# A transformer block on one core: feed-forward products taken in pairs that share one weight load

## The chip, the core and the metric

The kernel runs on one core of a Trainium2 chip. The core has a matrix engine (TensorE; in the profile PE for its products and PEld for its loads of the stationary operand), three engines for elementwise work (VectorE: DVE, ScalarE: ACT, GpSimd: POOL) and a sync engine (SP) that here issues every DMA. On-chip data lie in SBUF (128 partitions); products land in PSUM, eight banks of 512 fp32 columns by 128 partitions. The metric is the device time of the program in microseconds (us), the median over runs; lower is better.

## The reference, cut to what matters

A pre-normalised block on `x[1, 2048, 1024]`, bf16: a segment-wise attention with a memory (32 heads, four segments of 512 tokens), then a gated feed-forward part. The change touches the second.

```python
def _B_ref(x, w1, w3, w2):
    gate = jnp.einsum('bsd,df->bsf', x, w1)      # w1, w3: 1024 x 3584
    up = jnp.einsum('bsd,df->bsf', x, w3)
    h = _silu(gate) * up
    out = jnp.einsum('bsf,fd->bsd', h, w2)       # w2: 3584 x 1024
    return out
...
    h = x + _A_ref(_layernorm(x, axis=-1), A_wq, A_wk, A_wv, A_wo, A_beta)
    h2 = h + _B_ref(_layernorm(h, axis=-1), B_w1, B_w3, B_w2)
```

## The kernel before, in words

A matrix product on the PE has a stationary operand of 128x128, brought in by a weight load of its own, and a moving operand of up to 512 columns that streams past it. `mms` (L720) issues such products for one PSUM bank, by fours, in one operation of the kernel's graph; each `e.matmul` (L729) becomes a weight load (LDWEIGHTS) and a product (MATMUL) in the program.

The 2048 tokens of the feed-forward part are worked in two blocks of 1024 tokens (`blk` 0 and 1).

- `ffn_up` (L1457) takes 256 columns of `w1` and `w3` at a time (14 steps `ch`, two halves `jj` of 128 columns). For each 128 columns and for each of the block's two halves of 512 tokens (`tc`) it makes a gate product into one bank (eight 128x128 pieces of `w1` as stationary operand, the normalised tokens `hnT` as moving operand), an up product with `w3` into another, then a tanh on ACT (L1478) and two operations on DVE (L1481, L1486) that write 512 columns of the hidden tile `hm`. The two token halves use the same weight pieces, and each loads them for itself.
- `ffn_down` (L1490) goes over the block's eight tiles of 128 tokens. Tile `t` is 0 to 15 over both blocks. For each of two halves of 512 output columns it sums 28 products (a 128x128 piece of `hm` as stationary operand, 512 columns of `w2` as moving one), and DVE adds the residual (L1510, `ob<-hr,ps`), after which SP sends the result to `out` (DMA at L398). The two column halves use the same pieces of `hm`, and each loads them for itself. The last tile, 15, is cut into pieces of 512, 256, 128 and 128 columns.

The order of the work is written out. `ORDER` lists for each engine the numbers of the graph's operations, and `BANKS` the PSUM bank of each group of products; `schedule` (L414) reads them, and `emit` (L479) issues the operations in just that order, with a semaphore wait where one engine needs another's result or where a PSUM bank or an SBUF buffer must have become free. So an engine whose next operation in the list has to wait makes everything behind it in its list wait too. The lists mix the phases: products of the feed-forward part of block 0 stand between pieces of attention, and `ffn_down` of block 0 between products of `ffn_up` of block 1.

Outputs go through eight buffers `ob0` to `ob7`, and the residual rows through three buffers `hr0` to `hr2` (tile `t` uses `hr` number `t % 3`).

Of the kernel before, what the change touches and what calls it, by code (L numbers as in the profile page):

```python
# [190 lines left out]
    "5756756576575675675675675677565107316576556756756756756401646765645112176123477516566067"  # L191
    "1475126240464765741742104645620164175406601654602543517712717317717447771275715174547354"
    "7271767543567254614167726564776675635274511652665361546457121514574023412547765765674557"
    "405765"
# [381 lines left out]
class Kernel:  # L576
# [138 lines left out]
    def dense_group(self, late=False):  # L715
        g = Group([(5,), (6,), (7,)],
                  ("att", [(4,), (0,), (1,), (2,), (3,)]) if late else None, True)
        return g

    def mms(self, group, items, cls, split=4, eager=False):  # L720


        last = None
        for i in range(0, len(items), split):
            part = items[i:i + split]
            cost = sum(mm_ns(p[5]) for p in part)

            def emit(e, gr, part=part):
                return [e.matmul(p[0](gr), p[1], p[2], start=p[3], stop=p[4]) for p in part]  # L729

            used = part if eager or i else items
            last = self.g.op("pe", cost, emit, reads=[p[1] for p in used] + [p[2] for p in used],
                             cls=cls, group=group)
            last.mode = "full"
        return last
# [721 lines left out]
    def ffn_up(self, blk, ch):  # L1457
        self.g.stage()
        n = self.n_w13
# [140 lines left out]
```

## Time and profile before

| | |
|---|---|
| median of 3 runs | 883.27 us (883.24 to 883.63) |
| the profiled execution | 882.95 us |
| its span, first to last instruction | 881.1 us |
| PE busy | 876.6 us, 5789 products |
| PEld busy | 397.6 us, 5789 loads |
| DVE, ACT, POOL busy | 442.6, 300.9, 166.3 us |

The span is what the profile's views divide up; 1.85 us of the profiled execution lie around it. A view that merges equal instructions which follow each other gives their first start, the time from that start to the last one's end, and their count. The matmuls of such a row overlap (each has its own start, and an end that is modelled), so that the step from one to the next is the row's time less one duration, divided by the count less one.

### The profile page before, as it was taken

The numbers are of one execution on the slowest core, as the hardware profiler recorded it, in microseconds if no ns is written. First come the engines' busy times: TensorE is split into PE (matmuls) and PEld (weight loads), VectorE is DVE, ScalarE is ACT, GpSimd is POOL, SyncE is SP. The second block draws the span as 40 slices with busy tenths as digits, with TensorE's granted clock in tenths as the row PEclk, the third lists the DMA queues.
The fourth block names the chain that finished last, engine by engine and source line by source line (L and its number), as shares of the span: only waits on it lengthen the run. The fifth ranks groups of instructions, "written<-read, shape, count | busy, mean of one in ns | idle before, by whom it ended". The sixth has DMA issues, their size and how long they took to land.

```text
span 881.1 us, 13700 instructions
## 1 busy us (share of the span) xinstructions
PE 876.6 (99%) x5789; PEld 397.6 (45%) x5789; DVE 442.6 (50%) x749; ACT 300.9 (34%) x349; POOL 166.3 (19%) x231
## 2 busy tenths in 40 slices
PE   9999999999999999999999999999999999999998
PEld 5344444444444444444444444444444444444445
DVE  6777888886666687655354301322243344231011
ACT  4887676769656656511111000111011111110000
POOL 3534344335342534303000000000000000000000
PEclk9999999999999999999999999999999999999999
DMA  9879948556962727395483410311322322201011
GB/s 237 235 203 228 223 96 217 144 145 178 224 161 68 173 74 167 106 290 143 119 241 93 108 36 30 84 48 54 96 80 58 96 73 63 86 7 48 19 42 42
DMA packets 152140, 106.54 MB, mean 121 GB/s; under 512 B 49552, under 2 KB 137872, under 8 KB 151056
## 3 DMA queue, kind: packets, MB, share of 16 engines
q1 hardware_dynamic: 152080, 105.67, 45.8%
q8 instruction: 46, 0.75, 0.4%
q14 instruction: 14, 0.11, 0.0%
HBM read 84.94 MB, written 9.44 MB: 107 GB/s over the span
## 4 chain that ended last, share of the span: by engine, by line
PE 99%; DMA 0%; ACT 0%; SPq 0%; issue 0%; DVE 0%; DVEq 0%
PE ps L729 92%; PE ps L1188 3%; PE ps L1281 3%; DMA wp<-in_A_wq_dram 0%; PE ps L1109 0%; PE ps L1405 0%; ACT et L1202 0%; SPq L398 0%; PE ps L1274 0%; PE ps L741 0%; DVE ob L1510 0%; DVEq L534 0%
## 5 line engine op out<-in xcount | busy, mean ns | idle before, releaser
L729 PE MATMUL ps<-hnT,w1b 128*128 128x512 bf16 x896 | 216.2, 379 | 0.0
L729 PE MATMUL ps<-hnT,w3b 128*128 128x512 bf16 x896 | 213.9, 379 | 0.0
L729 PE MATMUL ps<-w2b,hm 128*128 128x512 bf16 (+2 forms) x952 | 199.2, 366 | 0.0
L1478 ACT ACTIVATE sg<-ps 128x512 bf16<-128x512 f32 x112 | 66.8, 597 | 385.4 <-PE ps L729 384.2
L1481 DVE SCALAR_TENSOR_TENSOR t<-sg,ps 128x512 bf16<-128x512 bf16 x112 | 76.6, 685 | 190.1 <-ACT sg L1478 189.9
L1202 ACT ACTIVATE et<-ps 128x2048 bf16<-128x2048 f32 x80 | 150.1, 1876 | 46.3 <-PE ps L1188 44.4
L729 PEld LDWEIGHTS ps<-w2b,hm 128*128 128x128 bf16 x952 | 90.8, 98 | 103.1 <-issue 0.3
L729 PEld LDWEIGHTS ps<-hnT,w1b 128*128 128x128 bf16 x896 | 86.4, 98 | 105.4 <-issue 5.3
L729 PEld LDWEIGHTS ps<-hnT,w3b 128*128 128x128 bf16 x896 | 86.4, 98 | 105.3 <-issue 3.1
L1211 POOL TENSOR_SCALAR_AFFINE_SELECT et<-et 128x512 bf16<-128x512 bf16 (+1 forms) x96 | 81.0, 856 | 104.3 <-ACT et L1202 104.2
L1486 DVE SCALAR_TENSOR_TENSOR hm<-t,ps 128x512 bf16<-128x512 bf16 x112 | 76.2, 684 | 43.5 <-PE ps L729 41.6
L1510 DVE TENSOR_TENSOR ob<-hr,ps 128x512 bf16<-128x512 bf16 (+2 forms) x34 | 21.9, 655 | 122.3 <-PE ps L729 122.2
L729 PE MATMUL ps<-wo,oT 128*128 128x512 bf16 x256 | 61.1, 380 | 0.0
L729 PE MATMUL ps<-hnT,wp 128*128 128x512 bf16 x256 | 59.7, 380 | 0.0
L729 PE MATMUL ps<-xnT,wp 128*128 128x512 bf16 (+1 forms) x256 | 51.5, 350 | 0.0
L1227 DVE TENSOR_TENSOR sum<-sum,et 128x512 bf16<-128x512 bf16 (+1 forms) x64 | 41.5, 657 | 3.6 <-POOL et L1211 1.7
L729 PEld LDWEIGHTS ps<-wo,oT 128*128 128x128 bf16 x256 | 23.8, 98 | 29.7 <-issue 3.0
L729 PEld LDWEIGHTS ps<-hnT,wp 128*128 128x128 bf16 x256 | 23.6, 98 | 29.7 <-issue 3.7
L729 PEld LDWEIGHTS ps<-xnT,wp 128*128 128x128 bf16 x256 | 21.8, 98 | 24.3 <-issue 2.6
L1188 PE MATMUL ps<-qT,kT 32*128 32x128 bf16 (+3 forms) x512 | 31.7, 301 | 0.2
L1450 DVE TENSOR_TENSOR h<-h,ps 128x512 bf16<-128x512 bf16 x32 | 21.7, 680 | 20.0 <-PE ps L729 19.6
L729 PE MATMUL ps<-wp,hnT 128*128 128x512 bf16 x128 | 30.4, 380 | 0.0
(126 smaller groups left out, 589.8 us busy)
## 6 DMA issues: line engine op xcount, KB each, us to landing
w1b<-in_B_w_dram SPq DMA_DIRECT2D x28, 512.0 KB, 4.1
w3b<-in_B_w_dram SPq DMA_DIRECT2D x28, 512.0 KB, 4.1
wp<-in_A_wv_dram SPq DMA_DIRECT2D x8, 1024.0 KB, 6.0
wp<-in_A_wq_dram SPq DMA_DIRECT2D x7, 1024.0 KB, 6.0
wp<-in_A_wk_dram SPq DMA_DIRECT2D x7, 1024.0 KB, 7.3
w2b<-in_B_w_dram SPq DMA_DIRECT2D x7, 1024.0 KB, 5.9
h<-in_A_x_dram SPq DMA_DIRECT2D x16, 256.0 KB, 3.3
h_scr<-h SPq DMA_DIRECT2D x16, 256.0 KB, 3.2
```

What stands on the lines that cost most here:

```text
L729: return [e.matmul(p[0](gr), p[1], p[2], start=p[3], stop=p[4]) for p in part]
L1188: ins.append(e.matmul(self.bank(gr, j, 512 - 128 * kc, off), k[r, g0 + g, 128 * kc:128 * kc + 128], q[r, g0 + g, 128 * kc:512], start=True ...
L1202: return [e.activation(et[:, :, :], src, AF.Exp, scale=self.scale)]
L1211: self.pool_op(lambda e, v=v, pat=pat: e.affine_select(v, v, pattern=pat, compare_op=ALU.is_ge, fill=0.0, base=0, channel_multiplier=-1), ...
L1227: lambda e, gr: [e.tensor_tensor(o, a, b, op=ALU.add) for o, a, b in sums],
L1281: ins.append(e.matmul(self.ps[32 * i:32 * i + 32, b * 512 + c0:b * 512 + c0 + n], lhsT(i, kc, j), rhs(i, j), start=kc == 0 and j == first, ...
L1450: self.g.op("dve", dve_ns(512), lambda e, gr, hs=hs: [e.tensor_tensor(hs, hs, self.bank(gr), op=ALU.add)], reads=[hs], writes=[hs], cls=1, ...
L1478: self.g.op("act", act_ns(512), lambda e, gr, sg=sg: [e.activation(sg, self.bank(gr), AF.Tanh, scale=0.5)], writes=[sg], cls=0, group=gg)
L1481: e.scalar_tensor_tensor(t1, sg, 1.0, self.bank(gr), op0=ALU.add, op1=ALU.mult)], reads=[sg], writes=[t1], cls=0,
L1486: e.scalar_tensor_tensor(dst, t1, 0.5, self.bank(gr), op0=ALU.mult, op1=ALU.mult)], reads=[t1], writes=[dst], cls=0,
L1510: self.g.op("dve", dve_ns(n), lambda e, gr, hs=hs, ob=ob, n=n: [e.tensor_tensor(ob, hs, self.bank(gr, 0, n), op=ALU.add)], reads=[hs], wri ...
```

## The change

Two products that use the same stationary operand are issued one behind the other, and the second is issued without a weight load. This is done for the gate and up products of block 1 (`both = blk`), where the pair is the two halves of 512 tokens, and for `ffn_down` of tiles 0 to 14, where the pair is the two halves of 512 columns. Block 0's gate and up products and tile 15's `ffn_down` stay as they were. A pair fills two banks side by side and both are done at the same time. `again` builds the product that has no load of its own. From operation 1738 on, the lists of the order (`ORDER`) and the banks (`BANKS`) are new for every engine.

```diff
     "act": (
...
     "dve": (
...
-        "2465-2466 2456-2457 2479-2480 2472-2473 2486-2487 2534 2496 2543 2505 2515 "
-        "2524 2591 2553 2600 2572 2581 2562 2610 2619 2629 2638 2647 2656"
+        "2456-2457 2454 2469-2470 2472 2483 2473 2484 2486-2487 2505 2503 2522 2524 2541 2543 "
+        "2562 2560 2579 2581 2638 2656 2600 2598 2629 2619 2617 2647"
...
-    def dense_group(self, late=False):
+    def dense_group(self, late=False, safe=True):
         g = Group([(5,), (6,), (7,)],
-                  ("att", [(4,), (0,), (1,), (2,), (3,)]) if late else None, True)
+                  ("att", [(4,), (0,), (1,), (2,), (3,)]) if late else None, safe)
         return g
...
+    def pairs(self, both, items, cls, eager=False):
+
+        last = None
+        for i in range(0, len(items), 2):
+            part = items[i:i + 2]
+
+            def emit(e, gr, part=part):
+                ins = []
+                for w, xs, first, end in part:
+                    for k, (g, x) in enumerate(zip(gr.parts, xs)):
+                        out = self.bank(g)
+                        ins.append(self.again(e, ins[-1], out, x) if k else
+                                   e.matmul(out, w, x, start=first, stop=end))
+                return ins
+
+            used = part if eager or i else items
+            last = self.g.op("pe", 2 * sum(mm_ns(512) for _ in part), emit,
+                             reads=[p[0] for p in used] + [x for p in used for x in p[1]],
+                             cls=cls, group=both)
+            last.mode = "full"
+        return last
+
+    def again(self, e, like, out, x):
+
+        m = like.ins
+        return e.add_instruction(mybir.InstMatmult(
+            name=self.nc.get_next_instruction_name(), engine=m.engine,
+            ins=[e.lower_ap(x), m.ins[1]], outs=[e.lower_ap(out)],
+            start_tensor_calc=m.start_tensor_calc, stop_tensor_calc=m.stop_tensor_calc,
+            tile_size=m.tile_size, tile_position=m.tile_position, ldweights=False))
...
+            both = blk
+            gs = [[self.dense_group(True, not both) for _ in range(2)] for _ in range(2)]
             for tc in range(2):
                 self.g.stage()
+                if both and not tc:
+                    for k, w in enumerate((w1, w3)):
+                        self.pairs(Both(gs[0][k], gs[1][k]), [
+                            (w[:, c, jj * 128:(jj + 1) * 128],
+                             [self.hnT[2 * blk + i][:, c, :] for i in range(2)], c == 0, c == 7)
+                            for c in range(8)], 7)
...
-                gg, gu = self.dense_group(True), self.dense_group(True)
-                for gr, w in ((gg, w1), (gu, w3)):
+                gg, gu = gs[tc]
+                for gr, w in () if both else ((gg, w1), (gu, w3)):
...
+            two = Both(*[self.dense_group(True) for _ in range(2)])
+            if t < 15:
+                self.pairs(two, [(self.hm[fc][:, i * 128:(i + 1) * 128],
+                                  [self.w2[fc // 4][:, fc % 4, c0:c0 + 512] for c0 in (0, 512)],
+                                  fc == 0, fc == 27) for fc in range(28)], 8, eager=True)
             for c0, n in cols:
-                gr = self.dense_group(True)
...
+                gr = two.parts[c0 // 512] if t < 15 else self.dense_group(True)
+                if t == 15:
...
```

How the new order stands on three engines, at three places. In the rows, a number behind a name is a buffer; `[waits ...]` names the semaphores an instruction waits for; line numbers are those of each version's own text (L729 before is L725 after, L1510 is L1551, L398 is L394; L745 is a pair's first product and L758 the second, without a load).

On PE, in block 1, products of `ffn_up` among those of `ffn_down` of an earlier tile (`hnT2` and `hnT3` are the block's token halves, `w1b1` a buffer of `w1`). Before:

```order
L729 MATMUL ps<-hnT2_127,w1b1_131 128x512 x4
L729 MATMUL ps<-w2b0_165,hm0_137 128x512
L729 MATMUL ps<-w2b0_165,hm1_138 128x512
L729 MATMUL ps<-w2b0_165,hm2_139 128x512
L729 MATMUL ps<-w2b0_165,hm3_140 128x512
L729 MATMUL ps<-hnT2_127,w1b1_131 128x512 x4
```

After:

```order
L745 MATMUL ps<-hnT2_127,w1b1_131 128x512
L758 MATMUL ps<-hnT3_128,w1b1_131 128x512
L745 MATMUL ps<-hnT2_127,w1b1_131 128x512
L758 MATMUL ps<-hnT3_128,w1b1_131 128x512
L745 MATMUL ps<-w2b0_165,hm0_137 128x512
L758 MATMUL ps<-w2b0_165,hm0_137 128x512
L745 MATMUL ps<-w2b0_165,hm1_138 128x512
L758 MATMUL ps<-w2b0_165,hm1_138 128x512
```

Four products of one token half that each loaded a piece became two pieces with two products each; the count of products is the same, and the interleaving of the two phases stays.

On DVE, the last additions of the program (`ob<-hr,ps`). `hr1` holds the residual of tile 13, `hr2` of tile 14 and `hr0` of tile 15, and of tile 12 in the first two rows of the second list. `ob1 ... 128x128` that closes the first list, and stands fourth in the second, is tile 15's last 128 columns. Before:

```order
L1510 TENSOR_TENSOR ob4_179<-hr2_174,ps 128x512 [waits s_pe,s_dma3,s_dma15]
L1510 TENSOR_TENSOR ob5_180<-hr2_174,ps 128x512 [waits s_pe]
L1510 TENSOR_TENSOR ob6_181<-hr0_172,ps 128x512 [waits s_pe]
L1510 TENSOR_TENSOR ob7_182<-hr0_172,ps 128x256 [waits s_pe]
L1510 TENSOR_TENSOR ob0_175<-hr0_172,ps 128x128 [waits s_pe]
L1510 TENSOR_TENSOR ob1_176<-hr0_172,ps 128x128 [waits s_pe]
```

After:

```order
L1551 TENSOR_TENSOR ob0_175<-hr0_172,ps 128x512 [waits s_pe]
L1551 TENSOR_TENSOR ob1_176<-hr0_172,ps 128x512
L1551 TENSOR_TENSOR ob7_182<-hr0_172,ps 128x256 [waits s_pe,s_dma11,s_dma10]
L1551 TENSOR_TENSOR ob1_176<-hr0_172,ps 128x128 [waits s_pe]
L1551 TENSOR_TENSOR ob3_178<-hr1_173,ps 128x512
L1551 TENSOR_TENSOR ob2_177<-hr1_173,ps 128x512
L1551 TENSOR_TENSOR ob6_181<-hr0_172,ps 128x512
L1551 TENSOR_TENSOR ob5_180<-hr2_174,ps 128x512
L1551 TENSOR_TENSOR ob4_179<-hr2_174,ps 128x512
L1551 TENSOR_TENSOR ob0_175<-hr0_172,ps 128x128
```

The addition of the last 128 columns was the last of the list and now has six others behind it, five of them of 512 columns; those six carry no wait of their own for PE.

On SP, the last DMAs of the program. Before:

```order
L398 DMA out_0_dram<-ob5_180 128x512 [waits s_dve]
L398 DMA out_0_dram<-ob6_181 128x512 [waits s_dve]
L398 DMA out_0_dram<-ob7_182 128x256 [waits s_dve]
L398 DMA out_0_dram<-ob0_175 128x128 [waits s_dve]
L398 DMA out_0_dram<-ob1_176 128x128 [waits s_dve]
```

After:

```order
L394 DMA out_0_dram<-ob5_180 128x512 [waits s_dve]
L394 DMA out_0_dram<-ob2_177 128x512
L394 DMA out_0_dram<-ob6_181 128x512
L394 DMA out_0_dram<-ob4_179 128x512 [waits s_dve]
L394 DMA out_0_dram<-ob7_182 128x256
L394 DMA out_0_dram<-ob0_175 128x128 [waits s_dve]
L394 DMA out_0_dram<-ob1_176 128x128
L394 DMA out_0_dram<-ob3_178 128x512
```

Five outputs each waited for an addition of their own; now the first of eight waits for the addition into `ob5`, the eighth row of DVE's second list, and seven others stand behind it.

More of the change, by code (lines that the diff above doesn't have):

```diff
@@ L190 @@
     "6765776560000076755675000000012473000000000000124730000000000001243000000000000124305665"
[L191 to L194, printed above, removed]
+    "5756756576575675675675675677565307536576556756756756756401646765645145677605477501563763"
+    "3405310214265720747056420113051374516305420123674501627340510627431567506132057423054673"
+    "2456013741023546327140326537142046750123456701547365407251426317645017235064125604723102"
+    "315476"
 )
@@ L1500, in ffn_down @@
             cols = [(0, 512), (512, 256), (768, 128), (896, 128)] if t == 15 else [(0, 512), (512, 512)]
-            for c0, n in cols:
-                gr = self.dense_group(True)
-                self.mms(gr, [(lambda gr, n=n: self.bank(gr, 0, n),
-                               self.hm[fc][:, i * 128:(i + 1) * 128],
-                               self.w2[fc // 4][:, fc % 4, c0:c0 + n],
-                               fc == 0, fc == 27, n) for fc in range(28)], 8, eager=True)
+            two = Both(*[self.dense_group(True) for _ in range(2)])
[3 more added lines that the diff above has]
+                                  fc == 0, fc == 27) for fc in range(28)], 8, eager=True)
+            for c0, n in cols:
+                gr = two.parts[c0 // 512] if t < 15 else self.dense_group(True)
+                if t == 15:
+                    self.mms(gr, [(lambda gr, n=n: self.bank(gr, 0, n),
+                                   self.hm[fc][:, i * 128:(i + 1) * 128],
+                                   self.w2[fc // 4][:, fc % 4, c0:c0 + n],
+                                   fc == 0, fc == 27, n) for fc in range(28)], 8, eager=True)
                 ob = self.ob[self.n_ob % 8][:, 0:n]
```

121 rows, old and new, of the table ORDER are left out of this document.

## The prediction

> **What bounds the kernel now.** First the page's busy times and its chain of waits, then the busy times of stretches.
>
> ```profile
> span 881.1 us, 13700 instructions
> ...
> PE 876.6 (99%) x5789; PEld 397.6 (45%) x5789; DVE 442.6 (50%) x749; ACT 300.9 (34%) x349; POOL 166.3 (19%) x231
> ...
> PEclk9999999999999999999999999999999999999999
> ...
> PE 99%; DMA 0%; ACT 0%; SPq 0%; issue 0%; DVE 0%; DVEq 0%
> ```
>
> ```profile
> 560.00:800.00 240.00, 240.00 (x1114) 108.76 (x1113) 80.87 (x119) 32.84 (x55) 0.00 (x0) 1.00 0.22 65
> 850.00:881.00 31.00, 28.70 (x188) 15.91 (x186) 3.66 (x7) 0.00 (x0) 0.00 (x0) 1.00 0.19 56
> ```
>
> The columns are the stretch, its length, the busy time and count of PE, PEld, DVE, ACT and POOL, the granted clock, and the DMAs. PE is the chain from start to end, at full clock. From 560 to 800 us, the block the change works on, it has no gap, while its weight loads fill 45%, DVE 34% and ACT 14%. But a busy PE is not a PE at its peak, so the step from product to product has to be read, at both widths there are at the end of the program. The first fence is from the timeline at 845 to 849 us, the second at 877.9 to 878.6, the third has durations from the groups by shape.
>
> ```profile
> 844.84 4.48 PE L729 MATMUL ps<-w2b,hm 128*128 128x512 bf16 x20
> 845.05 3.98 PEld L729 LDWEIGHTS ps<-w2b,hm 128*128 128x128 bf16 x19
> 845.68 1.88 DVE L1510 TENSOR_TENSOR ob<-hr,ps 128x512 bf16<-128x512 bf16 x3 [15.72 <-PE ps L729]
> ```
>
> ```profile
> 877.70 1.00 PE L729 MATMUL ps<-w2b,hm 128*128 128x128 bf16 x15
> ```
>
> ```profile
> L729 PE MATMUL ps<-w2b,hm 128*128 128x512 bf16 x868 | 193.5, 379 | 0.0
> ...
> L729 PE MATMUL ps<-w2b,hm 128*128 128x128 bf16 x56 | 4.1, 219 | 0.0
> ```
>
> ```profile
> L729 PEld LDWEIGHTS ps<-w2b,hm 128*128 128x128 bf16 x952 | 90.8, 98 | 103.1 <-issue 0.3
> ```
>
> 512 columns: (4.48 - 0.379) / 19 = 215.8 ns a step. 128 columns: (1.00 - 0.219) / 14 = 55.8 ns. The difference, 160.0 ns for 384 columns, is 0.417 ns a column, so 512 columns take 213.4 ns and 2.4 ns are left that do not depend on the width. A load takes 98 ns, and one comes with each product, at 55.8 ns steps too: loads run beside products and each other. Of a 512-column product with a load of its own, then, nearly everything is columns that a product without a load must stream too.
>
> The third place is the end of the program: the timeline at 876 to 882 us, and what waits there.
>
> ```profile
> 878.81 0.29 DVE L1510 TENSOR_TENSOR ob<-hr,ps 128x128 bf16<-128x128 bf16 x1 [1.24 <-PE ps L729]
> ```
>
> ```profile
> 879.12 0.33 SPq L398 DMA_DIRECT2D out_dram<-ob  x1
> ```
>
> ```profile
> DMA to landing us min/median/max: 1.5/1.5/1.6
> ```
>
> The last product is answered by one short addition, over at 879.10, and one DMA from 879.12 that lands 1.5 us later, at 880.6; about 0.5 us of closing follows up to 881.1. What follows the last addition takes 2.0 us (the last row is of the `ob` DMAs in that stretch).
>
> **The loads that go.** The second product of a pair loses its load. In block 1 that is 14 steps x 2 column halves x 2 (gate, up) x 8 = 448 products; in `ffn_down` 15 tiles x 28 = 420; together 868 of 5789. The trace has no product without a load, so its price is bounded. From below: it cannot cost less than its columns, 213.4 ns, which would save 868 x 2.4 ns = 2.1 us. From above: were the next piece's load no longer brought in beside a running product, each pair would show its 98 ns, 868 x 98 ns = 85 us more. I take 215.8 ns, the row of the same shape, so nothing: the 2.4 ns are the same at both widths and go with a product, and nothing in the rows ties them to the load. Both ends are kept below, as rivals.
>
> A rule bears on this choice. The Trainium skill, "TensorE: Matmul & The Clock Gate", section "Wait — 56ns, not 53.3ns?", calls about 2.5 ns a fixed cost of each matmul, behind its decoding; the trace agrees with the size (2.4 ns). By that rule the removed loads save 0; if the 2.4 ns belonged to the exchange of weights, 2.1 us. What no row here shows is which of the two it is.
>
> **Pairs and banks.** A pair finishes two banks at once. After a gate pair ACT has two tanh and DVE two operations, after an up pair DVE two more:
>
> ```profile
> L1478 ACT ACTIVATE sg<-ps 128x512 bf16<-128x512 f32 x112 | 66.8, 597 | 385.4 <-PE ps L729 384.2
> L1481 DVE SCALAR_TENSOR_TENSOR t<-sg,ps 128x512 bf16<-128x512 bf16 x112 | 76.6, 685 | 190.1 <-ACT sg L1478 189.9
> L1486 DVE SCALAR_TENSOR_TENSOR hm<-t,ps 128x512 bf16<-128x512 bf16 x112 | 76.2, 684 | 43.5 <-PE ps L729 41.6
> ```
>
> Gate banks are free 0.6 + 0.6 + 0.69 = 1.9 us after the pair's end, beneath the up pair's 16 x 0.216 = 3.45 us; the up banks after 2 x 0.68 = 1.4 us, beneath the next products in two to four other banks of the eight. I cost this at nothing; PE's products hide it. Where a pair's bank is wanted while one such DVE operation is still to come, PE waits up to 0.69 us; I keep one such wait, 0.7 us, for the upper end. The number of DVE, ACT and POOL operations, of DMAs, and the columns on PE do not change.
>
> **The end of the program.** Here the new lists cost. On DVE the addition of the last 128 columns has to wait for PE's last products, as before, but six additions stand behind it: of tile 13 (two), of tile 15's first 512 columns, of tile 14 (two), and of 128 columns. Tile 13's products, by the order on PE, were done well before. All six run after PE has ended. On SP eight outputs stand at the end, the first of which needs the addition into `ob5`, the fourth of 512 columns behind the short one.
>
> The row of 845.68 above has three such additions that don't wait: (1.88 - 0.69) / 2 = 0.60 us each. For DMAs that don't wait, SP at 871 us:
>
> ```profile
> 871.02 2.29 SPq L398 DMA_DIRECT2D out_dram<-ob  x5
> ```
>
> ```profile
> L398 SPq DMA_DIRECT2D out_dram<-ob x5: 333/449/452, 871.0 to 872.9; - x5
> ...
> DMA to landing us min/median/max: 1.7/1.8/1.8
> ```
>
> (2.29 - 0.45) / 4 = 0.46 us from issue to issue, and each of the five lands 1.8 us after its issue: they do not hold each other up. From the end of the short addition on:
>
> - four additions of 512 columns until `ob5` is there: 4 x 0.60 = 2.4 us;
> - seven further issues until the last of eight begins: 7 x 0.46 = 3.2 us (the additions into `ob4` and `ob0` are over 0.6 and 0.8 us after `ob5`, before their DMAs' turn at 1.4 and 2.3 us);
> - the last DMA, 128 KB, lands: 1.8 us;
> - closing: 0.5 us, as now.
>
> Together 7.9 us in place of 2.0: **5.9 us more**. Nothing covers it, since PE has ended.
>
> **Sum.** The profiled execution took 882.95 us, 0.3 less than the median of 883.27. 882.95 + 5.9 + 0 (loads) + 0 (banks) = 888.85; on the median, **889.2 us**. Its own range: 0.3 us for the rounding of 0.60 and 0.46 over eleven steps, 0.5 us for how early the first addition can start, 0.7 above for a wait on a bank: 888.4 to 890.2.
>
> **Rivals.**
>
> *The loads carry the 2.4 ns.* Then every product without a load takes 213.4 ns: 889.2 - 2.1 = 887.1 us. For it: each of the 5789 products had a load, so the rows can't separate the two. Against it: a load lasts 98 ns and is hidden even at 55.8 ns steps.
>
> *A load after a pair is no longer hidden.* The load for the next piece must pass two products instead of one. If it waits for the second to end, up to 98 ns show per pair, 889.2 + 85 = 974 us. For it: the trace has never had two products between loads. Against it: even if the load cannot start before the second product does, that one's 216 ns cover it twice.
>
> *Loads slow the products beside them, and fewer loads make up for the end.* This is the one on the other side: the step of 215.8 would hold more of the load than its fixed part. It decides from 5.9 us / 868 = 6.8 ns a product; if a product without a load streamed in half of 98 ns less, 868 x 49 ns = 42.5 us would go and the time be 889.2 - 42.5 = 847 us. For it: PEld is busy 45%. Against it: the slope of 0.417 ns a column is the same whether a load falls into every 56 or every 216 ns, which leaves no more than 2.4 ns.
>
> That the second product loads its weights all the same (5789 loads in the profile after) would leave the time at 889.2, since the loads were free; it stands with the forecast.
>
> **How the numbers follow.** Forecast 0.71, the first rival 0.18, the second 0.05, the third 0.06. The range takes in the forecast with its own range and the first rival with 0.7 below it: 886.4 to 890.4 us. A measurement of this kernel tells about 0.2% from no change, here 1.8 us: forecast and the first two rivals lie over that on the slow side, 0.94; of the third, 0.04 for faster and 0.02 for within, where it only balances the end.
>
> **What would show it.** Right: 4921 loads, a step of 215.8 ns in pairs; after PE's last product one short addition, six more without a pause, then eight DMAs 0.46 us apart, the last begun 5.6 us after the short addition; a span near 887. Wrong: steps of 213.4 ns (first rival), pairs with a gap of up to 98 ns (second), steps under 209 ns (third), idle time of PE before a pair that ends with a DVE operation (banks), or outputs issued before the short addition.

## The result and the profile after

The changed kernel takes 888.74 us (median), the kernel before 883.25 in the same set of runs; the ratio is 1.0063, with a 95% interval of 1.0044 to 1.0082. It is slower by 5.5 us, where 889.2 was forecast (888.4 to 890.2 as the forecast's own range, 886.4 to 890.4 with the first rival). The profiled execution took 888.64 us, its span 886.9.

The page after, and the stretch from 560 to 800 us in the columns explained above:

```profile
span 886.9 us, 12834 instructions
...
PE 876.6 (99%) x5789; PEld 312.6 (35%) x4921; DVE 437.2 (49%) x748; ACT 298.5 (34%) x350; POOL 167.0 (19%) x231
```

```profile
560.00:800.00 240.00, 240.00 (x1114) 54.38 (x557) 78.13 (x122) 30.68 (x56) 0.00 (x0) 1.00 0.22 64
```

868 loads are gone, and in block 1 half of them (557 in place of 1113). PE makes as many products in that stretch as before, 1114, and its busy time over the whole program is the same 876.6 us (busy time alone would not show it, since the ends of products are modelled; the count does). The removed loads are worth nothing. The timeline at 700 to 702 us shows why, product by product; L745 is the first of a pair, L758 the second, and behind a load stands how long the load engine idled before it:

```profile
700.21 0.38 PE L758 MATMUL ps<-hnT,w1b 128*128 128x512 bf16 x1
700.22 0.10 PEld L745 LDWEIGHTS ps<-hnT,w3b 128*128 128x128 bf16 x1 [0.34 <-issue]
700.43 0.38 PE L745 MATMUL ps<-hnT,w3b 128*128 128x512 bf16 x1
...
700.65 0.38 PE L758 MATMUL ps<-hnT,w3b 128*128 128x512 bf16 x1
700.65 0.10 PEld L745 LDWEIGHTS ps<-hnT,w3b 128*128 128x128 bf16 x1 [0.34 <-issue]
...
700.86 0.38 PE L745 MATMUL ps<-hnT,w3b 128*128 128x512 bf16 x1
```

From 700.21 to 700.86 lie three steps of 0.216 us, from second to first product (with a change of weights between them) and from first to second (without one) alike. Over the 240 us the starts in the trace give a mean step of 215.8 ns from first to second and of 215.9 ns from second to first; in the kernel before it is 215.8. The next piece's load starts with the second product and is over after 0.10 of its 0.216 us.

The time went to the end of the program. The timeline from 878 us, and the outputs in it:

```profile
878.19 0.39 PE L725 MATMUL ps<-w2b,hm 128*128 128x128 bf16 x4
878.62 3.47 DVE L1551 TENSOR_TENSOR ob<-hr,ps 128x128 bf16<-128x128 bf16 x7 [1.43 <-PE ps L725]
881.32 3.74 SPq L394 DMA_DIRECT2D out_dram<-ob  x8
```

```profile
L394 SPq DMA_DIRECT2D out_dram<-ob x8: 332/441/452, 881.3 to 884.6; - x8
...
DMA to landing us min/median/max: 1.5/1.8/1.9
```

PE's last products stand at about the same place as before (the short addition starts at 878.62 where it started at 878.81). Then DVE makes seven additions without a pause. SP issues nothing until 881.32, when the addition into `ob5` is there, and then eight outputs one behind the other. Before, the same place held one addition of 0.29 us and one output at 879.12.

### The profile page after: what moved, and what is told of

It is laid out like the page before. It is cut to its first block, busy times and chain, and to the rows that moved or that the text cites. A ratio compares the mean times of both kernels' runs of the same rounds, so it can differ in the third digit from the quotient of the medians.

```text
span 886.9 us, 12834 instructions
## 1 busy us (share of the span) xinstructions
PE 876.6 (99%) x5789; PEld 312.6 (35%) x4921; DVE 437.2 (49%) x748; ACT 298.5 (34%) x350; POOL 167.0 (19%) x231
## 4 chain that ended last, share of the span: by engine, by line
PE 98%; DMA 0%; DVE 0%; ACT 0%; SPq 0%; issue 0%; DVEq 0%
PE ps L725 49%; PE ps L745 21%; PE ps L758 21%; PE ps L1215 3%; PE ps L1308 3%; DMA wp<-in_A_wq_dram 0%; DVE ob L1551 0%; PE ps L1136 0%; PE ps L1432 0%; ACT et L1229 0%; SPq L394 0%; PE ps L1301 0%; PE ps L768 0%; DVEq L1592 0%
## 5 line engine op out<-in xcount | busy, mean ns | idle before, releaser
L1513 ACT ACTIVATE sg<-ps 128x512 bf16<-128x512 f32 x112 | 63.8, 596 | 390.1 <-PE ps L758 252.9
L745 PE MATMUL ps<-w2b,hm 128*128 128x512 bf16 x420 | 159.2, 379 | 0.0
L758 PE MATMUL ps<-w2b,hm 128*128 128x512 bf16 x420 | 159.2, 379 | 0.0
L725 PE MATMUL ps<-hnT,w1b 128*128 128x512 bf16 x448 | 108.9, 379 | 0.0
L725 PE MATMUL ps<-hnT,w3b 128*128 128x512 bf16 x448 | 108.4, 379 | 0.0
L1551 DVE TENSOR_TENSOR ob<-hr,ps 128x512 bf16<-128x512 bf16 (+2 forms) x34 | 20.7, 652 | 151.6 <-PE ps L758 116.9
L745 PEld LDWEIGHTS ps<-w2b,hm 128*128 128x128 bf16 x420 | 41.1, 98 | 136.2 <-issue 135.2
L745 PE MATMUL ps<-hnT,w3b 128*128 128x512 bf16 x224 | 84.9, 379 | 0.0
L758 PE MATMUL ps<-hnT,w3b 128*128 128x512 bf16 x224 | 84.9, 379 | 0.0
L758 PE MATMUL ps<-hnT,w1b 128*128 128x512 bf16 x224 | 84.9, 379 | 0.0
L745 PE MATMUL ps<-hnT,w1b 128*128 128x512 bf16 x224 | 84.9, 379 | 0.0
L725 PE MATMUL ps<-wo,oT 128*128 128x512 bf16 x256 | 62.1, 380 | 0.0
L725 PEld LDWEIGHTS ps<-hnT,w3b 128*128 128x128 bf16 x448 | 42.5, 98 | 52.8 <-issue 3.8
L725 PEld LDWEIGHTS ps<-hnT,w1b 128*128 128x128 bf16 x448 | 42.5, 98 | 53.0 <-issue 4.4
L725 PE MATMUL ps<-hnT,wp 128*128 128x512 bf16 x256 | 59.7, 380 | 0.0
L725 PE MATMUL ps<-xnT,wp 128*128 128x512 bf16 (+1 forms) x256 | 51.5, 350 | 0.0
L745 PEld LDWEIGHTS ps<-hnT,w1b 128*128 128x128 bf16 x224 | 21.9, 98 | 74.8 <-issue 73.6
L745 PEld LDWEIGHTS ps<-hnT,w3b 128*128 128x128 bf16 x224 | 21.9, 98 | 74.8 <-issue 74.1
```

The source lines that it names most:

```text
L745: e.matmul(out, w, x, start=first, stop=end))
L758: return e.add_instruction(mybir.InstMatmult(name=self.nc.get_next_instruction_name(), engine=m.engine, ins=[e.lower_ap(x), m.ins[1]], out ...
L1513: self.g.op("act", act_ns(512), lambda e, gr, sg=sg: [e.activation(sg, self.bank(gr), AF.Tanh, scale=0.5)], writes=[sg], cls=0, group=gg)
L1551: self.g.op("dve", dve_ns(n), lambda e, gr, hs=hs, ob=ob, n=n: [e.tensor_tensor(ob, hs, self.bank(gr, 0, n), op=ALU.add)], reads=[hs], wri ...
```

## The experiments

All of them edit the changed kernel, but for the last, which edits the kernel before. Each ratio is to the kernel before in the same set of runs, with its 95% interval. The median of the kernel before is 883.25 us in the set of the result, 883.31 in that of four of the experiments, and 882.94 in that of the other three (DVE's end, SP's end, both ends), so that a difference between medians of two sets is good to about 0.3 us.

### Loads given back

```diff
-                        ins.append(self.again(e, ins[-1], out, x) if k else
-                                   e.matmul(out, w, x, start=first, stop=end))
+                        ins.append(e.matmul(out, w, x, start=first, stop=end))
```

> The changed kernel with its lists and pairs as they are, but every second product of a pair loads its stationary operand again (5789 loads instead of 4921). Theory (a load beside a running product is free, the slowdown is all in the program's end): no change, 888.7 us within 0.3, step in the pairs still 215.8 ns. Rival (the 2.4 ns that do not depend on the width belong to the load): 868 x 2.4 ns = 2.1 us more, 890.8 us.

Measured: 888.72 us, ratio 1.0061 (1.0047 to 1.0075). The stretch from 560 to 800 us:

```profile
560.00:800.00 240.00, 240.00 (x1114) 108.58 (x1113) 78.08 (x122) 30.67 (x56) 0.00 (x0) 1.00 0.22 64
```

The loads are back (1113), the products are as many, the time is that of the changed kernel. The removal of loads by itself neither saves nor costs; the intervals of the two kernels overlap almost wholly, and a difference of 2.1 us (0.24%) between the medians, as the rival has it, is not there. The mean step in the stretch is 215.8 ns with the loads as without them.

### One load for four products

```diff
-                        ins.append(self.again(e, ins[-1], out, x) if k else
+                        ins.append(self.again(e, ins[-1], out, x, first, end) if ins else
                                    e.matmul(out, w, x, start=first, stop=end))
```

> The changed kernel with one weight load for four products: the second pair of each operation streams past the first pair's stationary operand (so that half of the pieces of w1, w3 and of the hidden tile are not used, and the output is another one). 434 further loads go, and three steps out of four have no exchange of weights before them. Theory (the 2.4 ns go with a product): 888.7 us, every step 215.8 ns. Rival (an exchange costs the 2.4 ns but is hidden or spread over a pair's two steps): 434 x 2.4 ns = 1.0 us less, 887.7 us, and steps of 213.4 ns within a four.

Measured: 889.29 us, ratio 1.0070 (1.0055 to 1.0086). The stretch, and the timeline in it:

```profile
560.00:800.00 240.00, 240.00 (x1114) 27.19 (x278) 78.08 (x122) 30.68 (x56) 0.00 (x0) 1.00 0.22 64
```

```profile
700.80 0.38 PE L745 MATMUL ps<-hnT,w3b 128*128 128x512 bf16 x1
701.02 0.81 PE L758 MATMUL ps<-hnT,w3b 128*128 128x512 bf16 x3
...
701.45 0.10 PEld L745 LDWEIGHTS ps<-hnT,w3b 128*128 128x128 bf16 x1 [0.77 <-issue]
...
701.67 0.38 PE L745 MATMUL ps<-hnT,w3b 128*128 128x512 bf16 x1
```

Four steps from 700.80 to 701.67 are 0.87 us, 0.217 each within the rounding of the rows, and (0.81 - 0.38) / 2 = 0.215 within a run of three products with no exchange of weights at all. Over the stretch the starts in the trace give 215.8 ns for the steps within a four and 215.9 for the step to the next four. With a quarter of the loads, 240 us hold the same 1114 products. So the 2.4 ns that do not depend on the width do not belong to the load or the exchange, at this width. The median is not below that of the changed kernel; what it lies above it (0.6 us, with overlapping intervals) is not told from nothing.

### DVE's end alone

```diff
-2562 2560 2579 2581 2638 2656 2600 2598 2629 2619 2617 2647
+2562 2560 2579 2581 2600 2598 2647 2638 2629 2619 2617 2656
```

> The changed kernel with DVE's last eight additions in the order in which PE finishes their products; SP's list as it is. Theory of the end: the addition into ob5 (tile 14) then waits for its pair, ends near 879.1 us instead of 881.3, and the same eight outputs follow it 0.47 us apart: last issue near 882.5, landing 1.8, closing 0.5, span near 884.8, 2.2 us less than the changed kernel: 886.5 us. Rival (the lists cost time in the middle, not at the end): 888.7 us.

Measured: 886.63 us, ratio 1.0045 (1.0030 to 1.0060), 2.1 us less than the changed kernel's median. The timeline of DVE and SP there:

```profile
878.44 1.48 DVE L1551 TENSOR_TENSOR ob<-hr,ps 128x512 bf16<-128x512 bf16 x3 [0.17 <-PE ps L758]
```

```profile
879.16 3.74 SPq L394 DMA_DIRECT2D out_dram<-ob  x8
```

The burst of eight is the same 3.74 us; it only starts 2.16 us earlier. What DVE's order costs is what it delays on SP.

### SP's end alone

```diff
-2561 2602 2580 2544 2542 2582 2620 2599 2630 2618 2639 2648 2657 2601
+2561 2602 2580 2544 2542 2582 2639 2657 2601 2599 2630 2620 2618 2648
```

> The changed kernel with SP's last eight outputs in the order of DVE's additions; DVE's list as it is. Theory of the end: every output but the last two leaves right behind its addition; the last addition ends at 882.1 us as in the changed kernel, its output of 32 KB is issued near 882.4 and lands 1.5 later, closing 0.5: span near 884.4, 2.5 us less: 886.2 us. Rival (SP's order is of no account, DVE alone sets the end): 888.7 us.

Measured: 886.93 us, ratio 1.0042 (1.0026 to 1.0058), a median 0.7 us above what was expected. The profiled execution (887.73 us) lies higher still, and shows the end and what was lost ahead of it. DVE and SP at the end:

```profile
880.22 3.47 DVE L1551 TENSOR_TENSOR ob<-hr,ps 128x128 bf16<-128x128 bf16 x7 [1.43 <-PE ps L725]
```

```profile
878.82 5.51 SPq L394 DMA_DIRECT2D out_dram<-ob  x8
```

The additions run as in the changed kernel, 1.60 us later on the clock, and the outputs now go out beside them: the last issue ends at 884.33, 0.64 us after the last addition (883.69), where it was 2.97 us in the changed kernel (885.06 and 882.09). That is the 2.3 us gained at the end, and the last output is now a short one. The 1.60 us were lost earlier. The first exponential of the attention, and one at 152 us, in the changed kernel:

```profile
20.18 1.88 ACT L1229 ACTIVATE et<-ps 128x2048 bf16<-128x2048 f32 x1 [0.77 <-PE ps L1215]
```

```profile
152.45 1.88 ACT L1229 ACTIVATE et<-ps 128x2048 bf16<-128x2048 f32 x1 [1.47 <-PE ps L1215]
```

The same two here:

```profile
21.00 1.88 ACT L1229 ACTIVATE et<-ps 128x2048 bf16<-128x2048 f32 x1 [0.77 <-PE ps L1215]
```

```profile
153.71 1.88 ACT L1229 ACTIVATE et<-ps 128x2048 bf16<-128x2048 f32 x1 [1.47 <-PE ps L1215]
```

They are 0.82 and 1.26 us later, in a stretch of the program that none of the edits touches. At 400 us the lag is 1.49. What PE waited for up to 300 us shows most of it. The rows give the time in all, the number of waits and the longest: 0.2 us for transfers of attention weights in the changed kernel, then 1.2 and 0.3 here:

```profile
PE ps L725 <- DMA wp<-in_A_wq_dram: 0.2, 1, 0.2
```

```profile
PE ps L725 <- DMA wp<-in_A_wq_dram: 1.2, 3, 0.5
...
PE ps L725 <- DMA wp<-in_A_wk_dram: 0.3, 1, 0.3
```

So this execution lost time to transfers far ahead of its end, and its end is as much shorter as was expected (the table of ends below). How much of the median's 0.7 us such waits explain was not measured.

### Both ends

The two edits together, SP's list now `... 2542 2582 2601 2599 2648 2639 2630 2620 2618 2657`.

> Both edits: DVE's last additions and SP's last outputs in the order in which PE finishes. PE's list stays, so tile 14's pair still ends only 0.2 us before PE's last product. Theory of the end: additions into ob5 and ob4 and the short one end near 879.1, 879.7 and 880.0 us, the last output (32 KB) is issued near 880.2, span near 882.2, 4.7 us less than the changed kernel: 884.0 us. Rival (middle): 888.7 us.

Measured: 884.30 us, ratio 1.0021 (1.0007 to 1.0036). 4.4 us of the 5.5 are back. What is left hangs on PE's list: tile 14's pair ends just before PE does, and its two additions of 512 columns, with the short one behind them, come after it (PE's last product starts at 877.99):

```profile
878.02 1.48 DVE L1551 TENSOR_TENSOR ob<-hr,ps 128x512 bf16<-128x512 bf16 x3 [0.17 <-PE ps L758]
```

### PE's end too

```diff
-2651 2627 2613 2634 2614 2652-2654 2635 2645 2615 2636 2646 2637 2628 2616 2655
+2651 2627 2613 2634 2614-2616 2628 2635-2637 2645-2646 2652-2655
```

DVE's list then ends on `2600 2598 2619 2617 2629 2638 2647 2656`, SP's on `2601 2599 2620 2618 2630 2639 2648 2657`.

> The changed kernel with DVE's last additions and SP's last outputs in the order in which PE finishes, and on PE the last products of tile 14's pair brought forward, so that the program ends on tile 15's narrow pieces as the kernel before does. Theory: after PE's last product only the short addition, one issue, 1.5 us of landing and 0.5 of closing remain; PE itself ends 0.1 us earlier than in the kernel before: span near 880.9, 882.7 to 883.2 us, the same as before within 0.1%. Rival (pairs, by taking two banks at once, or the missing loads cost or save time in the middle): over 884.5, or under 882.

Measured: 882.54 us, ratio 0.9994 (0.9986 to 1.0003): the same as the kernel before. The end, on DVE and on SP:

```profile
879.10 0.29 DVE L1551 TENSOR_TENSOR ob<-hr,ps 128x128 bf16<-128x128 bf16 x1 [0.60 <-PE ps L725]
```

```profile
876.30 3.44 SPq L394 DMA_DIRECT2D out_dram<-ob  x6
```

One short addition to 879.39 and one output behind it, whose issue ends at 879.74; a span of 881.4 (this execution, of 883.11 us, lies 0.6 over the median). With pairs, 868 fewer loads and new lists everywhere else, this is the time before, within the interval. So no loss or gain in the middle can be told. It is the best version of this study, but not one that can be told from the kernel before.

### The kernel before, with a late end

```diff
-2524 2591 2553 2600 2572 2581 2562 2610 2619 2629 2638 2647 2656
+2524 2591 2553 2600 2572 2581 2562 2629 2638 2656 2610 2619 2647
...
-2573 2621 2554 2602 2563 2611 2601 2582 2592 2620 2630 2639 2648 2657
+2573 2621 2554 2602 2563 2582 2620 2601 2592 2611 2630 2639 2648 2657
```

> The kernel before, without pairs, given an end like that of the changed kernel: on DVE the addition of the last 128 columns stands ahead of three others (two of 512 columns, one of 128), on SP the output of tile 14's second half stands ahead of seven others. Theory of the end: 2 x 0.60 us until that output can be issued, 7 x 0.46 us of issues, 1.5 to 1.8 us of landing, 0.5 of closing: 6.4 to 6.7 us after the short addition in place of 2.0, 887.7 to 888.0 us. Rival (pairs or their new lists elsewhere make the time): 883.3 us.

Measured: 888.03 us, ratio 1.0053 (1.0039 to 1.0066), 4.7 us more than before (883.31). Its end:

```profile
878.50 1.68 DVE L1510 TENSOR_TENSOR ob<-hr,ps 128x128 bf16<-128x128 bf16 x4 [1.44 <-PE ps L729]
```

```profile
880.01 3.75 SPq L398 DMA_DIRECT2D out_dram<-ob  x8
```

Two edited lists make most of the loss without a single pair in the kernel.

## Why the prediction was right

**What bounds it, and the loads.** The step with a load of its own (215.8 ns) was taken for the product without one, and 2.1 us kept as a rival. The same count of products in 240 us with 1113, 557 and 278 loads, and steps that are alike within pairs and between them, show that the choice was right. The first rival (0.18) is refuted at this width. By the rule of the Trainium skill that was weighed ("TensorE: Matmul & The Clock Gate", "Wait — 56ns, not 53.3ns?") the fixed cost goes with each matmul; the runs agree (a step of 215.8 ns with every count of loads).

**The second rival** had the next load wait for the pair's second product. It does: it starts with that product and not with the first (the 0.34 us of idle load engine). But 0.10 us of load lie within 0.216 us of product, so that none of it shows, as the working against it had said.

**The third rival** needed 6.8 ns a product; the steps of 215.8 and 215.9 ns, for 215.8 before, leave nothing of it.

**Pairs and banks** were costed at nothing, with 0.7 us for one wait. In the changed kernel's trace the pairs run from 488.9 us to the end, and between two products in that time no step is longer than 0.24 us, so that no pair waited for a bank. The version with the end mended stands at 0.9994 of the kernel before, so that pairs and lists together do between 1.2 us less and 0.3 more outside the end.

**The end**, term by term, from the end of the short addition (878.62 + 0.28 = 878.90, where it was 879.10 before):

| term | predicted | measured |
|---|---|---|
| until the output of `ob5` can be issued | 2.4 | 881.32 - 878.90 = 2.4 |
| from the first to the last of eight issues | 3.2 | 3.74 - 0.43 = 3.3 |
| landing of the last one | 1.8 | 1.8 (median of the eight) |
| closing (what the span leaves) | 0.5 | 886.9 - 878.9 - 7.5 = 0.5 |
| together | 7.9 | 8.0 |

Against 2.0 before that is 6.0 more, and PE's end 0.2 us earlier leaves the 5.8 us between the spans, for 5.9 predicted. Those 0.2 us were not forecast and are chance: from execution to execution the spans of the kernel before differ by more.

The experiments show that it is these terms and not others. By the medians, DVE's list alone gives 2.1 us back (2.2 expected), SP's alone 1.8 (2.5), both lists 4.4 (4.7), all three 6.2 (5.5 to 6.0), and the kernel before loses 4.7 (4.4 to 4.7) from two such lists. A median also holds what executions lose ahead of the end. The traces tell the two apart, in us:

| version | PE's last product starts | span | from there to the end |
|---|---|---|---|
| before | 878.48 | 881.11 | 2.6 |
| changed | 878.36 | 886.93 | 8.6 |
| DVE's end | 878.41 | 884.77 | 6.4 |
| SP's end | 879.96 | 885.99 | 6.0 |
| both ends | 877.99 | 881.79 | 3.8 |
| PE's end too | 878.84 | 881.38 | 2.5 |
| before, late end | 878.18 | 885.40 | 7.2 |

Read so, the four mended ends are 2.2, 2.5, 4.8 and 6.0 us shorter than that of the changed kernel, as their terms said (2.2, 2.5, 4.7 and 6.0), and the late end is 4.6 us longer than the one before. But for the execution that fell behind, PE's last product starts within 0.9 us of the same time in all of these, with pairs and without.

The forecast's 889.2 is 0.5 us over the median: 0.1 from the terms, 0.1 because 1.74 us lie around the span and not 1.85, and 0.2 because the median is 0.1 over the profiled execution where 0.3 was put on for it. One sum of the prediction does not come out: the forecast's own range ends at 890.2, so that the range that takes it in should end there too and not at 890.4. Nothing hangs on it.

## What to carry to other kernels

A weight load that runs beside a product of 512 columns cost nothing here, and leaving it out saved nothing; before such a change, read the step between products at two widths and see how much of it does not grow with the columns. Where lists are made anew, read their last rows on every engine first: an operation that waits for the last result of all should have nothing behind it in its list, since what stands there can start only then (here four of six additions and seven further issues lay bare, while the last two additions ran beside the issues), and each DMA that is left over at the end costs another issue of about 0.47 us. Where an engine is 99% busy, look for a loss in its own steps and behind its last one.

## What the runs showed of the hardware

The load for the next stationary operand does not run ahead as soon as the load engine is free. In the changed kernel it starts together with the product just ahead of its own (load at 700.65, the product ahead of it at 700.65, its own at 700.86), after 0.34 us of idle, and with one load for four products after 0.77 us. The kernel before shows the same lead of one product where the names change: the first load of a piece of `w3` starts at 700.23, its product at 700.44.

```profile
700.23 1.82 PEld L729 LDWEIGHTS ps<-hnT,w3b 128*128 128x128 bf16 x9
700.44 1.89 PE L729 MATMUL ps<-hnT,w3b 128*128 128x512 bf16 x8
```

Outputs that follow each other do not hold each other up: eight issued 0.47 us apart each land 1.5 to 1.9 us after their own issue, where one alone (128 KB, at 847.6 us in the kernel before) took 1.7, so that such a burst costs its issues and one landing.
